# Decode attention with a Mish layer: w2 loaded into one buffer in eighteen loads, wo's last load moved ahead of the last values

## The chip, the cores and the metric

The kernel runs on one core of a Trainium2 chip. The metric is the device time of one execution in microseconds (us); lower is better. Three runs of the kernel before gave a median of 1326.32 us (1326.3 to 1327.66). The profile is of one more execution, of 1326.37 us, on the same core.

## The reference, cut to what matters

The input is one token for each of eight sequences (x is 8 x 512). It is normalised, and then goes through two branches whose results are added to it.

```python
xn = layernorm(x)                                    # 8 x 512
# A: attention over a cache, 32 query heads, 8 key/value heads, 8192 positions, head size 128
q = (xn @ wq).reshape(8, 32, 128)
p = softmax(q . k_cache / sqrt(128))                 # four query heads share one k/v head
a = (p . v_cache).reshape(8, 4096) @ wo              # wo: 4096 x 512
# B: a dense layer, Mish, a dense layer
h = xn @ w1 + b1                                     # 8 x 1792
b = (h * tanh(softplus(h))) @ w2                     # w2: 1792 x 512
out = x + a + b
```

All arrays are float32. The caches hold 2 x 268 MB, the four weight matrices 24 MB together. Each byte is read once.

## The kernel before, in words

**The stream of loads.** Nearly everything that the kernel reads goes through one pool `kv` of four buffers of 128 partitions x 32 KiB (4 MiB; `buffer()`, line 87). A list `items` (lines 605 to 622) holds, in order, pairs of a load and the work on what it loaded. The loop at line 625 issues the load of the item three places ahead (`AHEAD`), then emits the work of the present item. All these loads are issued by SyncE (SP in the profile), in that order. A load into a buffer waits until the work on the buffer's previous content is done.

The framework gives each load one of eight completion semaphores, called lanes, in turn. A load on a lane follows the load eight before it on the same lane.

**The order of items.** The attention goes in 16 packs of four batch elements for one k/v head. Pack p's keys are loaded in four items of 4 MiB (`load_k`), interleaved with the values of pack p - 1 (`load_v`, 4 MiB each). wq comes in four items of 2 MiB spread over the run, w1 in one of 3.5 MiB near the start. wo comes in four items of 2 MiB (`wo_work`): the item for heads n and n + 1 (n = 0, 2, 4, 6) stands right behind a values item. At the end stand: the last keys, the values of pack 15 in four items (b = 0 to 3), wo's last item (n = 6), and w2 in three items of 2, 1 and 0.5 MiB, each with a buffer of its own.

**The work of an item.** `scores` multiplies keys by expanded queries (line 316). `maximum`, `weights` and `sums` make the softmax of a pack. `values` (line 385) multiplies weights by one values item, in two halves of 16 matmuls (line 394) with a `yield` between them, and then VectorE adds four column groups of the result into `os` (lines 404 and 406). `merge` (line 417) sums `os` over partitions on TensorE (line 421); for the last b of a pack VectorE writes the pack's part of `oT` (line 425). `outputs` (line 431) multiplies two heads' groups of `oT` by wo: 32 matmuls, each two passes in the profile (line 446), into PSUM tile M, and VectorE adds M to the accumulator `acc` (line 456). `mish` makes the activations `aT` early in the run. `down` (line 508) multiplies `aT` by rows of w2, four matmuls for each of 14 row blocks j, accumulated in PSUM tile H (line 512; two passes each as well). At the end VectorE adds H and `acc` into `res` (line 634), and SP stores it (line 635).

**Work put off.** `after(k, f)` has f run after k more steps, and a step is taken at each `yield`. So `merge` comes two steps after the second half of its values, and `outputs` three steps after its item. VectorE and TensorE run their instructions in the order in which they are emitted (lines 638 to 650).

**What the change and the prediction touch:** `load_w2` (130), `outputs` (431), `down` (508), `wo_work` (591), `w2_work` (598), the list of items (605 to 622).

Of the kernel before, what the change touches and what calls it, by code (L numbers as in the profile page):

```python
# [13 lines left out]
P = 128  # L14
B = 8
D = 512
HKV = 8
REP = 4
# [9 lines left out]
BW = 1024  # L28
# [4 lines left out]
Q = P // G  # L33
# [5 lines left out]
PACKS = HKV * NP  # L39
# [18 lines left out]
W2R = G * FT // 2 * FP // P  # L58
# [6 lines left out]
def kernel(  # L65
# [12 lines left out]
    nc = tc.nc  # L78
# [8 lines left out]
    def buffer():  # L87
        return kv.tile([P, NB * BW], F32, name="kv")

    def load_blocks(src, lo, n):  # L90

        _, rows, width = src.shape
        t = buffer()[:rows, : n * width].rearrange("p (j f) -> p j f", j=n)
        nc.sync.dma_start(t, src[lo : lo + n].rearrange("j p f -> p j f"))
        return t

    def batch_blocks(src, p, b):
        n, hb = divmod(p, NP)
        lo = ((hb * PB + b) * HKV + n) * NB
        return src[lo : lo + NB]  # L100

    def load_k(p, b):
        src = batch_blocks(kT, p, b)
        t = buffer()
        if p > 0:
            nc.sync.dma_start(
                t, src.rearrange("j p f -> (j p f)").rearrange("(p f) -> p f", p=P)
            )
            return t
        t = t.rearrange("p (j f) -> p j f", j=NB // KA)  # L110
        nc.sync.dma_start(
            t,
            src.rearrange("(j a) p f -> j (a p f)", a=KA).rearrange("j (p f) -> p j f", p=P),
        )
        return t

    def load_v(p, b):

        t = buffer().rearrange("p (s f) -> p s f", s=NH)
        nc.sync.dma_start(  # L120
            t,
            batch_blocks(v, p, b)
            .rearrange("(s j) p f -> s (j p f)", s=NH)
            .rearrange("s (p f) -> p s f", p=P),
        )
        return t

    w2_rows = w2.rearrange("j p f -> (j p) f").rearrange("(q i) f -> q (i f)", i=W2R)

    def load_w2(lo, hi):  # L130

        t = buffer()[:, : (hi - lo) * BW]
        nc.sync.dma_start(t, w2_rows[:, lo * BW : hi * BW])
        return t

    x_sb = const.tile([B, D], F32, name="x_sb")
# [5 lines left out]
    items = []  # L142
# [4 lines left out]
    M = psum.tile([P, 512], F32, name="m")  # L147
    H = psum.tile([P, 512], F32, name="h")
# [21 lines left out]
    acc = const.tile([P, P], F32, name="acc")  # L170
# [214 lines left out]
    def values(p, b, vt):  # L385


        o = O[b % 2]
        for s in range(NH):
            u = s * PB + b  # L390
            for k in range(W // W4 // G):
                for c in range(G):
                    j = G * k + c
                    nc.tensor.matmul(  # L394
                        o[Q * c : Q * c + W4 * REP, :],
                        PT[p][:, W4 * R * j + u : W4 * R * (j + 1) : U],
                        vt[:, s, 512 * j : 512 * (j + 1)],
                        start=(s == 0 and k == 0),
                        stop=(s == NH - 1 and k == W // W4 // G - 1),
                    )  # L400
            if s == 0:
                yield
        os = OS[p, b] = work.tile([P, DH], F32, name="os", bufs=3)
        nc.vector.tensor_scalar(os, o[:, :DH], isel[:, 0:1], None, op0=ALU.mult)  # L404
        for i in range(1, W4):
            nc.vector.scalar_tensor_tensor(  # L406
                os,
                o[:, DH * i : DH * (i + 1)],
                isel[:, i : i + 1],
                os,  # L410
                op0=ALU.mult,
                op1=ALU.add,
            )
# [3 lines left out]
    def merge(p, b):  # L417

        n, hb = divmod(p, NP)
        at = 168 + b * REP  # L420
        nc.tensor.matmul(M[:, at : at + REP], OS.pop((p, b)), hsel, start=True, stop=True)  # L421
        if b == PB - 1:
            if hb == 0:
                oT[n] = work.tile([P, REP, B], F32, name="oT", bufs=4)
            nc.vector.tensor_mul(  # L425
                oT[n][:, :, hb * PB : (hb + 1) * PB],
                M[:, 168 : 168 + REP * PB].rearrange("p (b h) -> p h b", h=REP),
                RT.pop(p),
            )

    def outputs(n, w):

        if n == 0:

            for g in range(G):
                nc.tensor.matmul(
                    M[Q * g : Q * g + B, 256:384],
                    ident[:B, :B],
                    x_sb[:, g * P : (g + 1) * P],
                    start=True,  # L440
                    stop=False,
                )
        for h in range(2 * REP):
            for g in range(G):
                at = h % 2 * D + g * P
                nc.tensor.matmul(  # L446
                    M[Q * g : Q * g + B, 256:384],
                    oT[n + h // REP][:, h % REP, :],
                    w[:, h // 2, at : at + P],
                    start=(h == 0 and n > 0),  # L450
                    stop=(h == 2 * REP - 1),
                )
        if n == 0:
            nc.vector.tensor_copy(acc, M[:, 256:384])
        else:
            nc.vector.tensor_add(acc, M[:, 256:384], acc)

    def mish(w1_sb):

# [48 lines left out]
    def down(lo, hi, w):  # L508
        for j in range(2 * lo, 2 * hi):
            for g in range(G):  # L510
                at = (j - 2 * lo) * D + g * P
                nc.tensor.matmul(  # L512
                    H[Q * g : Q * g + B, :P],
                    aT[:, j, :B],
                    w[:, at : at + P],
                    start=(j == 0),
                    stop=(j == 2 * W2R - 1),
                )
# [4 lines left out]
    def after(k, f):  # L523
        late.append([k, f])
# [9 lines left out]
    def wq_item(i):  # L534
        def spread(n):
            return spread_q(n, KR, NB, qc[:, n % 4])

        def work_on(t):
            for n in (2 * i, 2 * i + 1):
                project(n, t)  # L540
            if i == 0:
                spread_q(0, KA, KA, qc0)()
                spread(0)()
                spread(1)()
            else:
                even = spread(2 * i)

                def then():
                    even()
                    after(1, spread(2 * i + 1))  # L550

                after(2, then)
            yield

        return lambda: load_blocks(wq, i * CC, CC), work_on
# [5 lines left out]
    def k_work(p, b):  # L561
        def work_on(t):
            if (p, b) == (0, 0):
                expand(0)
            yield from scores(p, b, t)
            if b == 0 and p + 1 < PACKS:
                expand(p + 1)
            if b == PB - 1:

                def largest():  # L570
                    maximum(p)
                    after(1, exponents)

                def exponents():
                    lsel = weights(p)
                    after(3 if p < PACKS - 1 else 2, lambda: sums(p, lsel))

                after(3 if 0 < p < PACKS - 1 else 2, largest)
            yield

        return work_on

    def v_work(p, b):
        def work_on(t):
            yield from values(p, b, t)
            after(2, lambda: merge(p, b))
            yield

        return work_on

    def wo_work(n):
        def work_on(t):
            after(3, lambda: outputs(n, t))
            yield

        return work_on

    def w2_work(lo, hi):
        def work_on(t):
            down(lo, hi, t)  # L600
            yield

        return work_on

    setup()
    items.append(wq_item(0))
    for i in range(PB * PACKS + PB):
        p, b = divmod(i, PB)
        if p < PACKS:

            if b == 2 and p % (2 * NP) == 2 and p < PACKS - NP:
                items.append(wq_item(p // (2 * NP) + 1))
            if i == 2:
                items.append((lambda: load_blocks(w1, 0, 2 * CC), w1_work))
            items.append((lambda p=p, b=b: load_k(p, b), k_work(p, b)))
        if p > 0:
            items.append((lambda p=p, b=b: load_v(p - 1, b), v_work(p - 1, b)))
            if i > PB and (i - PB + 1) % (2 * NP * PB) == 0:
                n = (p - 1) // NP - 1
                items.append((lambda n=n: load_blocks(wo, n * 2, 4), wo_work(n)))  # L620
    for lo, hi in ((0, 4), (4, 6), (6, 7)):
        items.append((lambda lo=lo, hi=hi: load_w2(lo, hi), w2_work(lo, hi)))

    tiles = {}
    for i in range(-AHEAD, len(items)):
# [12 lines left out]
    last = {}  # L638
# [50 lines left out]
```

## Time and profile before

| | |
|---|---|
| median of three runs | 1326.32 us |
| the profiled execution | 1326.37 us |
| its span, first to last instruction | 1324.6 us |
| TensorE clock granted, mean | 0.974 |
| read from memory | 561 MB, 424 GB/s over the span |
| TensorE busy | 1194.0 us, 90% |
| VectorE busy | 230.8 us, 17% |

In the profile PE is TensorE's matmuls, PEld its weight loads, DVE VectorE, ACT ScalarE, and SPq the issues of SP. A timeline row has its start in us from the span's start, the time from the first start to the last end, the engine, the line, the operation, what it writes and reads, and the count; in brackets stands how long the engine was idle before it, and what ended that. Rows of the chain of waits have a start, a length and what the time went to. A row of a window has its length, each engine's busy time with its count of instructions, TensorE's granted clock, DMA's busy share and GB/s. A row of a DMA queue has packets, MB and its share of the sixteen engines' time.

### The profile page before, as it was taken

Reading aid. Unit: us, or ns where it says so; the run is one execution under the profiler, and the core shown is the slowest. Engines: PE = TensorE matmul, PEld = TensorE weight load, DVE = VectorE, ACT = ScalarE, POOL = GpSimd, SP = SyncE. Lnnn points to the kernel's source line nnn. Section 1 sums busy time; section 2 is a strip of 40 time slices with the busy share of each in tenths; the row PEclk is TensorE's granted clock in tenths of the full one; section 3 lists DMA queues with packets and bytes.
Section 4 is the critical chain, followed back from the end, with each engine's and each line's share of the span. In section 5 each row is a group of like instructions: output and inputs, shape, how many; then the busy total and the mean of one; then the engine's idle time right before and its main releaser. Section 6 shows DMA issues by size and latency. Waiting matters only on the chain.

```text
span 1324.6 us, 11226 instructions
## 1 busy us (share of the span) xinstructions
PE 1194.0 (90%) x5096; PEld 498.4 (38%) x5096; DVE 230.8 (17%) x620; ACT 24.6 (2%) x39; POOL 8.7 (1%) x10
## 2 busy tenths in 40 slices
PE   4999989998979998999998999899898898999885
PEld 3233344433334434333333434443343343333322
DVE  4320211202021021110201111120110201202021
ACT  1000000000000000000000000000000000000000
POOL 2000000000000000000000000000000000000000
PEclk9999989999989998999998999899999899999988
DMA  9999999999999999999999999999999999999997
GB/s 383 425 434 424 431 429 427 431 427 428 430 426 428 433 426 433 427 426 430 431 427 429 427 427 428 429 430 432 427 428 425 425 430 431 427 433 426 428 428 295
DMA packets 34071, 561.80 MB, mean 424 GB/s; under 512 B 2268, under 2 KB 2400, under 8 KB 7656
## 3 DMA queue, kind: packets, MB, share of 16 engines
q1 hardware_dynamic: 34000, 561.06, 99.5%
q8 instruction: 40, 0.66, 0.2%
q14 instruction: 7, 0.06, 0.0%
q10 hardware_dynamic: 24, 0.02, 0.0%
HBM read 561.01 MB, written 0.07 MB: 424 GB/s over the span
## 4 chain that ended last, share of the span: by engine, by line
PE 52%; DMA 46%; DVE 1%; issue 0%; ACT 0%; ACTq 0%
DMA kv<-in_kT 44%; PE s L316 41%; PE o L394 6%; DMA kv<-in_w 2%; PE h L252 1%; PE s L304 1%; PE m L446 1%; PE h L512 0%; DVE e L188 0%; PE m L421 0%; PE h L229 0%; DVE qs L242 0%; PE m L359 0%; DVE pt L367 0%; DVE oT L425 0%
## 5 line engine op out<-in xcount | busy, mean ns | idle before, releaser
L316 PE MATMUL s<-kv,qT 128*128 128x512 f32 x1920 | 874.2, 609 | 81.3 <-DMA kv<-in_kT 81.3
L316 PEld LDWEIGHTS s<-kv,qT 128*128 128x128 f32 x1920 | 361.8, 194 | 532.8 <-issue 452.6
L394 PE MATMUL o<-kv,pt 128*16 128x512 f32 x2048 | 239.2, 606 | 14.5 <-DMA kv<-in_v 9.7
L404 DVE TENSOR_SCALAR os<-o,isel 128x128 f32<-128x128 f32 x64 | 22.4, 351 | 600.3 <-PE o L394 600.3
L394 PEld LDWEIGHTS o<-kv,pt 128*16 128x16 f32 x2048 | 59.2, 111 | 168.6 <-issue 151.6
L406 DVE SCALAR_TENSOR_TENSOR os<-o,isel,os 128x128 f32<-128x128 f32 x192 | 67.3, 350 | 6.8
L327 DVE TENSOR_REDUCE nm<-s 128x1 f32<-128x1024 f32 x16 | 19.6, 1225 | 208.9 <-PE s L316 206.2
L366 ACT ACTIVATE e<-s,nmx 128x1024 f32<-128x1024 f32 x16 | 17.8, 1114 | 1204.3 <-DVE nmx L361 1204.3
L421 PEld LDWEIGHTS m<-hsel,os 128*128 128x128 f32 x128 | 23.6, 192 | 39.3 <-issue 29.8
L367 DVE STREAM_TRANSPOSE pt<-e 128x1024 f32<-128x1024 f32 x16 | 32.2, 2010 | 21.2 <-ACT e L366 21.2
L304 PE MATMUL s<-kv,qT 128*64 128x512 f32 x128 | 30.7, 639 | 2.5 <-DMA kv<-in_kT 1.4
L277 DVE TENSOR_SCALAR qT<-qc,bsel 128x128 f32<-128x128 f32 x120 | 30.6, 339 | 0.0
L421 PE MATMUL m<-hsel,os 128*128 128x4 f32 x128 | 19.3, 221 | 6.5 <-DVE nr L338 4.8
L252 PE MATMUL h<-psel,qs 128*128 128x32 f32 x132 | 19.5, 307 | 3.6 <-DVE qs L242 3.6
L252 PEld LDWEIGHTS h<-psel,qs 128*128 128x128 f32 x132 | 19.6, 229 | 7.3 <-DVE qs L242 4.4
L304 PEld LDWEIGHTS s<-kv,qT 128*64 128x64 f32 x128 | 10.0, 147 | 22.3 <-issue 20.0
L381 DVE RECIPROCAL r<-m 128x16 f32<-128x16 f32 x16 | 4.1, 257 | 71.4 <-PE m L377 71.4
L259 DVE COPY qc<-h 128x256 f32<-128x256 f32 (+1 forms) x9 | 3.6, 402 | 55.5 <-PE h L252 55.5
L202 PE MATMUL m<-ident,e 8*128 8x8 f32 x4 | 0.6, 247 | 12.4 <-DVE e L200 12.4
L242 DVE TENSOR_SCALAR qs<-h 128x1024 f32<-128x1024 f32 (+1 forms) x9 | 10.2, 1130 | 3.4 <-PE h L229 3.4
L229 PE MATMUL h<-kv,xnT 128*8 128x128 f32 x256 | 9.4, 309 | 0.3 <-DVE xnT L205 0.3
L425 DVE TENSOR_TENSOR oT<-m,r 128x16 f32<-128x16 f32 x16 | 2.7, 171 | 38.1 <-PE m L421 38.1
(80 smaller groups left out, 119.5 us busy)
## 6 DMA issues: line engine op xcount, KB each, us to landing
kv<-in_kT SPq DMA_DIRECT2D x64, 4096.0 KB, 24.7
kv<-in_v SPq DMA_DIRECT2D x64, 4096.0 KB, 30.0
kv<-in_wq SPq DMA_DIRECT2D x4, 2048.0 KB, 19.5
kv<-in_wo SPq DMA_DIRECT2D x4, 2048.0 KB, 20.1
kv<-in_w SPq DMA_DIRECT2D x1, 3584.0 KB, 36.6
kv<-in_w SPq DMA_DIRECT2D x1, 2048.0 KB, 24.9
kv<-in_w SPq DMA_DIRECT2D x1, 1024.0 KB, 16.8
kv<-in_w SPq DMA_DIRECT2D x1, 512.0 KB, 8.0
```

The costliest lines, as they stand in the source:

```text
L252: nc.tensor.matmul(H[:, r * R : (r + 1) * R], qs[:, r].rearrange("p g i -> p (g i)"), psel.rearrange("p h b -> p (h b)"), start=True, stop ...
L277: nc.vector.tensor_scalar(t[:, :, :, lo : lo + R - U + 1 : U], q, bsel[:, j : j + 1], None, op0=ALU.mult)
L304: nc.tensor.matmul(sp[WK * z : WK * (z + 1), cols], t[:, w : w + WK], k[:, NH * s + z, at : at + 512], start=(b == 0 and s == 0 and i == 0 ...
L316: nc.tensor.matmul(sp[:, cols], t[:, w : w + P], k[:, at : at + 512], start=(b == 0 and r == 0), stop=(b == PB - 1 and r == KR - 1),)
L327: nc.vector.tensor_reduce(NM[p], sp, axis=AX.X, op=ALU.max, negate=True)
L366: nc.scalar.activation(e, S[p % 2], AF.Exp, bias=nmx, accum_out=l)
L367: nc.vector.transpose(pt.rearrange("p (m t r) -> p t m r", m=m, t=TG), e.rearrange("p (t q m) -> p t m q", t=TG, m=m),)
L394: nc.tensor.matmul(o[Q * c : Q * c + W4 * REP, :], PT[p][:, W4 * R * j + u : W4 * R * (j + 1) : U], vt[:, s, 512 * j : 512 * (j + 1)], sta ...
L404: nc.vector.tensor_scalar(os, o[:, :DH], isel[:, 0:1], None, op0=ALU.mult)
L406: nc.vector.scalar_tensor_tensor(os, o[:, DH * i : DH * (i + 1)], isel[:, i : i + 1], os, op0=ALU.mult, op1=ALU.add,)
L421: nc.tensor.matmul(M[:, at : at + REP], OS.pop((p, b)), hsel, start=True, stop=True)
L446: nc.tensor.matmul(M[Q * g : Q * g + B, 256:384], oT[n + h // REP][:, h % REP, :], w[:, h // 2, at : at + P], start=(h == 0 and n > 0), st ...
```

## The change

Four things change, all at the end of the list of items.

- w2 is one item with one buffer. It is loaded by eighteen loads: the first 3/7 of each partition's row (1.5 MiB in all) in sixteen loads of eight partitions each, the next 3/7 in one load of 128 partitions, the last 1/7 in another.
- Where wo's last item stood behind the last values item, it stands ahead of it.
- wo's last products are not put off by three steps. They are emitted between w2's first and second part.
- They are accumulated in H, with w2's products, and not in M; the addition of M to `acc` for them goes.

```diff
-    def load_w2(lo, hi):
-
-        t = buffer()[:, : (hi - lo) * BW]
-        nc.sync.dma_start(t, w2_rows[:, lo * BW : hi * BW])
+    W2_PARTS = ((0, 3), (3, 6), (6, 7))
+
+    def load_w2():
+
+        t = buffer()[:, : W2R * BW]
+        for lo, hi in W2_PARTS:
+            cols = slice(lo * BW, hi * BW)
+
+            step = 8 if lo == 0 else P
+            for q in range(0, P, step):
+                nc.sync.dma_start(t[q : q + step, cols], w2_rows[q : q + step, cols])
         return t
...
     def outputs(n, w):
 
+        last = n == HKV - 2
+        to = H[:, :P] if last else M[:, 256:384]
...
                 nc.tensor.matmul(
-                    M[Q * g : Q * g + B, 256:384],
+                    to[Q * g : Q * g + B, :],
                     oT[n + h // REP][:, h % REP, :],
                     w[:, h // 2, at : at + P],
-                    start=(h == 0 and n > 0),
-                    stop=(h == 2 * REP - 1),
+                    start=(h == 0 and 0 < n and not last),
+                    stop=(h == 2 * REP - 1 and not last),
                 )
...
-        else:
-            nc.vector.tensor_add(acc, M[:, 256:384], acc)
+        elif not last:
+            nc.vector.tensor_add(acc, to, acc)
...
+    wo_last = []
+
     def wo_work(n):
         def work_on(t):
-            after(3, lambda: outputs(n, t))
+            if n == HKV - 2:
+                wo_last.append(t)
+            else:
+                after(3, lambda: outputs(n, t))
             yield
...
-    def w2_work(lo, hi):
-        def work_on(t):
+    def w2_work(t):
+        for lo, hi in W2_PARTS:
             down(lo, hi, t)
             yield
+            if lo == 0:
+
+                outputs(HKV - 2, wo_last[0])
...
-            items.append((lambda p=p, b=b: load_v(p - 1, b), v_work(p - 1, b)))
             if i > PB and (i - PB + 1) % (2 * NP * PB) == 0:
                 n = (p - 1) // NP - 1
-                items.append((lambda n=n: load_blocks(wo, n * 2, 4), wo_work(n)))
-    for lo, hi in ((0, 4), (4, 6), (6, 7)):
-        items.append((lambda lo=lo, hi=hi: load_w2(lo, hi), w2_work(lo, hi)))
+                wo_item = (lambda n=n: load_blocks(wo, n * 2, 4), wo_work(n))
+                v_item = (lambda p=p, b=b: load_v(p - 1, b), v_work(p - 1, b))
+                items += [wo_item, v_item] if p == PACKS else [v_item, wo_item]
+            else:
+                items.append((lambda p=p, b=b: load_v(p - 1, b), v_work(p - 1, b)))
+    items.append((load_w2, w2_work))
```

In `down` the column of a block j of w2 is counted from the start of the whole row, not of a part. The emitted order of TensorE at the end is then: the third values item of pack 15 and its merge, the last values item, w2's first part (24 matmuls), the last merge, wo's last products (32), w2's second part (24) and its third (8).

More of the change, by code (lines that the diff above doesn't have):

```diff
@@ L446, in outputs @@
                 nc.tensor.matmul(
-                    M[Q * g : Q * g + B, 256:384],
+                    to[Q * g : Q * g + B, :],
                     oT[n + h // REP][:, h % REP, :],
                     w[:, h // 2, at : at + P],
-                    start=(h == 0 and n > 0),
-                    stop=(h == 2 * REP - 1),
+                    start=(h == 0 and 0 < n and not last),
+                    stop=(h == 2 * REP - 1 and not last),
                 )
         if n == 0:
-            nc.vector.tensor_copy(acc, M[:, 256:384])
-        else:
-            nc.vector.tensor_add(acc, M[:, 256:384], acc)
+            nc.vector.tensor_copy(acc, to)
+        elif not last:
+            nc.vector.tensor_add(acc, to, acc)
     def mish(w1_sb):
@@ L510, in down @@
             for g in range(G):
-                at = (j - 2 * lo) * D + g * P
+                at = j * D + g * P
                 nc.tensor.matmul(
@@ L589, in v_work @@
         return work_on
+    wo_last = []
     def wo_work(n):
         def work_on(t):
-            after(3, lambda: outputs(n, t))
+            if n == HKV - 2:
+                wo_last.append(t)
+            else:
+                after(3, lambda: outputs(n, t))
             yield
         return work_on
-    def w2_work(lo, hi):
-        def work_on(t):
+    def w2_work(t):
+        for lo, hi in W2_PARTS:
             down(lo, hi, t)
             yield
-        return work_on
+            if lo == 0:
+                outputs(HKV - 2, wo_last[0])
     setup()
```

## The prediction

> **What bounds the kernel now.** I read the page's sections 1 to 4 first, then the chain of waits over the last 40 us, then the order in time of TensorE and of SP's issues there.
>
> ```profile
> span 1324.6 us, 11226 instructions
> PE 1194.0 (90%) x5096; PEld 498.4 (38%) x5096; DVE 230.8 (17%) x620; ACT 24.6 (2%) x39; POOL 8.7 (1%) x10
> ...
> DMA  9999999999999999999999999999999999999997
> ...
> q1 hardware_dynamic: 34000, 561.06, 99.5%
> q8 instruction: 40, 0.66, 0.2%
> q14 instruction: 7, 0.06, 0.0%
> q10 hardware_dynamic: 24, 0.02, 0.0%
> HBM read 561.01 MB, written 0.07 MB: 424 GB/s over the span
> ```
>
> The sixteen DMA engines are busy in every slice but the last, and SP's queue q1 takes 99.5% of their time: one stream of 561 MB at 424 GB/s. TensorE is 90% busy but waits for data whenever it has caught up. The change touches neither the bytes nor anything ahead of the last dozen loads, so it can win or lose only at the end of the stream.
>
> ```profile
> 1290.20 24.92 DMA kv<-in_w
> 1315.12 0.04 issue
> 1315.16 4.41 PE h L512 x96
> 1319.57 1.75 PE m L446 x64
> 1321.32 0.49 PE h L512 x16
> 1321.81 0.02 issue
> 1321.83 0.29 DVE res L634
> ```
>
> The chain ends on w2's first load (issued at 1290.20, landed at 1315.12). Behind it stand 6.65 us of TensorE work, then the result's addition and store. What can be gained is a part of these 6.65 us.
>
> ```profile
> 1295.38 3.20 PE L394 MATMUL o<-kv,pt 128*16 128x512 f32 x16 [5.24 <-DMA kv<-in_v]
> ...
> 1305.19 3.41 PE L394 MATMUL o<-kv,pt 128*16 128x512 f32 x16 [4.44 <-DMA kv<-in_v]
> 1308.53 0.39 PE L421 MATMUL m<-hsel,os 128*128 128x4 f32 x2
> 1308.85 1.93 PE L394 MATMUL o<-kv,pt 128*16 128x512 f32 x16
> 1312.40 0.39 PE L421 MATMUL m<-hsel,os 128*128 128x4 f32 x2 [1.63 <-DVE os L406]
> ```
>
> The last two values loads release TensorE at 1295.38 and 1305.19. The last one's products end at 1310.78. From the last values to w2's first part, 1305.19 to 1315.16, the stream moves wo's 2 MiB and 2 MiB of w2: 4.98 us for each 2 MiB.
>
> **The change, part by part.**
>
> *wo ahead of the last values.* wo takes the place of the last values in the queue and the other way round; both have their buffers in time, as SP's issues show (the pair ends at 1274.80, the next goes at 1285.86; by then the second last values and wo are still ahead, some 14 us of transfer).
>
> ```profile
> 1270.49 4.31 SPq L120 DMA_DIRECT2D kv<-in_v  x2
> ...
> 1285.86 0.37 SPq L94 DMA_DIRECT2D kv<-in_wo  x1
> 1290.20 20.96 SPq L133 DMA_DIRECT2D kv<-in_w  x3
> ```
>
> So the last values land one wo later: 1305.19 + 4.98 = **1310.17**. Their products take 3.41 + 1.93 = 5.34 us; the merge that stood between the halves moves forward into the wait for the values and costs nothing there (TensorE is idle from 1302 on). They end at 1315.5, 4.7 us later than now. This is the price of the move. What it buys: wo's products (1.75 us) no longer need anything late, and w2's products no longer start on a TensorE that has idled: now 96 take 4.41 us, 46 ns each, while the 64 behind them take 1.75, 27.3 ns each.
>
> *One buffer and sixteen pieces.* All 18 loads of w2 share one buffer, free at 1290.20. By the three rows above they could queue at once, 15 us before they are needed. But the compiled order of the changed kernel shows a wait on the DMA lanes (there are eight, taken in turn, and a load waits for the one eight before it on its lane):
>
> ```
> 135 L94 DMACopy kv<-in_wo 128x4x1024 [waits DMAHW5_49,PE_49]
> 136 L120 DMACopy kv<-in_v 128x2x4096 [waits DMAHW6_49,PE_49]
> 137 L140 DMACopy kv<-in_w 8x3072 [waits DMAHW7_49,PE_49]
> 138 L140 DMACopy kv<-in_w 8x3072 x4
> 139 L140 DMACopy kv<-in_w 8x3072 [waits DMAHW0_49]
> 140 L140 DMACopy kv<-in_w 8x3072 [waits DMAHW1_49]
> 141 L140 DMACopy kv<-in_w 8x3072 [waits DMAHW2_49]
> ```
>
> Counting pieces 0 to 15, piece 5 waits for the second last values, piece 6 for wo, and **piece 7 for the last values**. SP issues in order, so pieces 7 to 15 and w2's other two loads, 11 issues, all stand behind 1310.17. On SP nothing but the store is queued behind them; who waits is TensorE. That the stream is then empty for about a microsecond is new.
>
> The price of an issue: the nearest rows are SP's three w2 loads now and ACT's two small loads of eight and four partitions.
>
> ```profile
> L133 SPq DMA_DIRECT2D kv<-in_w x3: 328/341/341, 1290.2 to 1310.8; - x3
> ...
> 0.74 0.43 SPq L94 DMA_DIRECT2D kv<-in_wq  x1
> 1.23 1.04 SPq L111 DMA_DIRECT2D kv<-in_kT  x2
> ...
> 0.73 0.60 ACTq L137 DMA_DIRECT2D x_sb<-in_x  x1
> 1.37 0.26 ACTq L139 DMA_DIRECT2D b_sb<-in_b  x1
> ```
>
> With the 0.06 us gap between SP's first two issues, the ends are 0.26 + 0.06 = 0.32 and 0.60 + 0.06 = 0.66 us a piece. I take 0.40, from SP's own 0.34.
>
> The price of a piece's transfer: q10 carried just those two small loads, and its 24 packets are 8 + 4 rows and 8 + 4 completions. So a load of eight partitions runs on eight engines: 12 KiB each, at 424 / 16 = 26.5 GB/s 0.46 us. The store of the result gives the fixed part:
>
> ```profile
> out<-res SPq DMA_DIRECT2D x1, 64.0 KB, 1.6
> ```
>
> 64 KB on sixteen engines landed 1.6 us after the issue, so a lone piece (0.3 us more data per engine) lands after 1.9. Piece 7 goes out at 1310.2 and lands at 1312.1; eight more at 0.46 (more than the 0.40 of an issue) land by **1315.8**. With 0.66 us an issue it is 1310.2 + 8 x 0.66 + 1.9 = 1317.4.
>
> *The tail, summed.* The values' products end at 1315.5, the pieces are there at 1315.8, eight lanes are waited for at one instruction (0.2 us allowed): w2's first 48 products start at 1316.0 and end 48 x 27.3 ns later, 1317.3. The last merge is ready 1.62 us after the values' products (now 1310.78 to 1312.40), at 1317.1, hidden by them; 0.39 us, to 1317.7. wo's 64 products, 1.75 us, to 1319.45; the first half doesn't need the merge, which hides the 0.17 us multiplication behind it. w2's second load is issued at 1310.2 + 9 x 0.40 = 1313.8; on the engines that carry pieces it follows them: 1315.8 + 1.57 MB / 424 GB/s (3.7) = 1319.5. One more thing falls here: instruction fetches.
>
> ```profile
> q8 instruction: 1, 0.02, 2.7%
> ```
>
> This is the row of fetches among the DMA's of 1316 to 1318.5 now: one fetch, when TensorE has entered w2's products, on an engine with little left to do. TensorE reaches the same instructions at 1316 in the changed kernel, when every engine is in w2's second load. A fetch holds its engine for 0.2% x 16 x 1324.6 / 40 = 1.06 us; a load lands with its slowest engine. On an engine without pieces: 1313.8 + 1.6 + 3.5 (3.7 less what the 1.6 holds) + 1.06 = **1320.0**. So the second 48 products run 1320.0 to 1321.3, w2's third load (0.52 MB, 1.24 us) lands at 1321.25, the last 16 products (0.49) end at 1321.8. Now they end at 1321.81. **The sum is a change of 0.0 us**, with 0.1 for rounding up waits: the profiled execution's 1326.37 us (span 1324.6 and 1.8 around it; the three timed runs' median is 1326.32) becomes **1326.5 us**. The addition of wo's products to the accumulator, which goes, was hidden beside w2's last 16 products and gives nothing.
>
> **A rule against it.** The Trainium skill, "DMA: Bandwidth & Descriptors", section "Rules for kernel authors", asks for an outer dimension that is a multiple of 16, since one of fewer than 16 confines a load to that many engines. The section "Why a DMA increments its semaphore by 16 and not by 1" adds that SP's loads take the lowest-numbered ones. The packets of q10 agree with the first; which engines they are, no row shows. Spread over all sixteen by that rule, a piece would take 0.23 us, all would land by 1315.2, and the products, which wait for the values until 1315.5, would start 0.3 us sooner (an estimate). It is the third rival below.
>
> **The rivals.** About 0.2% (2.65 us) is what a measurement of this kernel can tell from no change; the bounds of the chances are 1323.7 and 1329.0.
>
> 1. *The lane waits and the fetch are hidden, and TensorE's own order is the bound.* From 1315.5: 1.31, the merge to 1317.5, 1.75, 1.31, 0.49: 1321.1, so -0.7 us, **1325.6**. For it: pieces and products meet within 0.3 us. Against: w2's second load is then needed at 1319.3, and by its rate alone comes at 1319.5. If the pieces were all queued early (the lane waits not being what I read), it is the same time, for the values land no sooner. Chance 0.28.
> 2. *SP's issues become the bound (the slower side).* At 0.66 us an issue w2's second load goes out at 1316.1 and lands at 1322.3 with the fetch, the third at 1323.6: end 1324.1, **1328.7**. Over 0.70 us an issue it is slower by over 0.2%; at 0.85 it is 1330.4. For it: ACT's 0.60 for eight partitions. Against: that was ACT's first, and four partitions took 0.26. Chance 0.15, half of it beyond 1329.
> 3. *The pieces fall on the late engines.* Engines finish apart: in 1310 to 1312 only 65% are busy, at 256 GB/s, while w2's first part is not yet down.
>
> ```profile
> 1308.00:1310.00 2.00, 2.00 (x18) 0.72 (x18) 0.00 (x0) 0.00 (x0) 0.00 (x0) 0.93 0.99 412
> 1310.00:1312.00 2.00, 0.77 (x8) 0.00 (x0) 1.05 (x3) 0.00 (x0) 0.00 (x0) 1.00 0.65 256
> ```
>
> If the eight engines with pieces are those that bring the last values last, pieces 0 to 6 (7 x 0.46 = 3.2 us) still stand there at 1310.2: all land by 1317.6 + 0.4, w2's others at 1321.7 and 1322.95, or 1.06 later with a fetch: **1328.1 to 1329.2**. Chance 0.10.
> 4. *The last values come earlier than by a whole wo*, since the late engines are what sets their landing and something relieves them: 3 us of that would make **1323.5**. No row shows what would. Chance 0.05.
>
> **How the numbers follow.** Forecast 0.42, rivals 0.28, 0.15, 0.10, 0.05. The likeliest is 1326.5; its own spread, 1325.9 to 1327.4. The range for 8 in 10 takes in rival 1 and most of 2 and 3: **1325.2 to 1329.3**. Faster by over 0.2%: rival 4 and little else, 0.05. Slower: half of rival 2, a third of 3, and 0.06 for prices that I have too low: 0.17. Within 0.2%: 0.78.
>
> **What would show it.** In the changed profile: TensorE waits for the last values until about 1310.2 instead of 1305.2; SP's small loads stand in two groups, the later one starting when the last values land, about 0.4 us apart; DMA's share drops around 1311; w2's products run at about 27 ns each; the last wait before the end is on w2's second load. Wrong would be: all sixteen pieces issued near 1290; issues over 0.7 us apart; last values before 1309; any difference ahead of 1290, where the two kernels issue the same loads.

## The result and the profile after

Four runs of the changed kernel have a median of **1337.72 us** (1336.93 to 1339.03), four runs of the kernel before on the same chip 1326.31 us (1326.24 to 1327.66): a ratio of 1.0084, 95% interval 1.0072 to 1.0097. The forecast was 1326.5 us, with no change as the likeliest case; the measured time is 8 us above its range. The profiled execution took 1338.47 us, so its terms stand 0.75 us above the median.

The head and the end of section 3 of the page after:

```profile
span 1336.7 us, 11241 instructions
...
HBM read 561.01 MB, written 0.07 MB: 420 GB/s over the span
```

The same bytes in a span that is 12.1 us longer (1336.7 less 1324.6). Up to 1290 the windows of the two kernels agree (DMA's GB/s to within 1). All of the loss lies in the last 45 us, which the chain of waits shows (start, length, what):

```profile
1285.13 27.01 DMA kv<-in_v
1312.14 0.02 issue
1312.15 3.89 DMA kv<-in_w
1316.05 0.02 issue
1316.06 10.12 DMA kv<-in_w
1326.18 0.20 issue
1326.38 2.75 PE h L521 x48
1329.12 0.52 PE m L428 x2
1329.64 2.42 PE h L455 x64
1332.07 1.80 PE h L521 x64
```

The last values land at 1312.14 (forecast 1310.17). Then comes piece 7, which waited for them (issued at 1312.15, landed at 1316.05), then piece 15, which waited for piece 7's lane (issued at 1316.06, landed at 1326.18, forecast 1315.8). w2's first products start at 1326.38 (forecast 1316.0), and TensorE ends at 1333.87 (forecast 1321.8): 10.4 us too late at the pieces, another 1.7 in the products behind them.

SP's waits from 1300 on (total, times, longest) stand on the instructions that the prediction named:

```profile
SPq L140 <- DMA kv<-in_v: 11.4, 1, 11.4
SPq L140 <- DMA kv<-in_wo: 4.8, 1, 4.8
SPq L140 <- DMA kv<-in_w: 2.7, 4, 0.8
```

One piece waits for wo, one for the last values, and all behind it with them. The last row is new: pieces 14 and 15 and w2's other two loads also waited for pieces 6 to 9, which should have been down long before, and so the last issues stand 0.8 to 1.1 us apart.

The windows show why. The columns are those of the prediction's rows; the last two are DMA's busy share and GB/s.

```profile
1303.00:1306.00 3.00, 0.39 (x2) 0.30 (x2) 0.21 (x1) 0.00 (x0) 0.00 (x0) 1.00 0.92 225
1306.00:1309.00 3.00, 0.00 (x0) 0.00 (x0) 0.00 (x0) 0.00 (x0) 0.00 (x0) 0.65 0.66 232
...
1312.00:1316.00 4.00, 3.82 (x20) 0.84 (x24) 0.00 (x0) 0.00 (x0) 0.00 (x0) 0.50 0.49 104
1316.00:1318.00 2.00, 2.00 (x16) 0.29 (x8) 0.00 (x0) 0.00 (x0) 0.00 (x0) 0.72 0.40 74
...
1320.00:1326.00 6.00, 0.00 (x0) 0.00 (x0) 0.00 (x0) 0.00 (x0) 0.00 (x0) 0.54 0.95 158
```

The first of these windows in the kernel before:

```profile
1303.00:1306.00 3.00, 0.81 (x4) 0.16 (x8) 0.00 (x0) 0.00 (x0) 0.00 (x0) 0.81 1.00 416
```

Read the last two columns together. From 1303 to 1306 the engines are 92% busy and move 225 GB/s, where the kernel before moved 416 at 100%. A busy engine that moves half as much isn't short of work: each of its packets takes longer. The trace's packet records show it: the values' packets of 16 KiB take 0.61 us in the kernel before, and in the changed kernel 0.90 us at the median of those that start from 1302 to 1304 and 1.17 from 1304 to 1306. From 1312 to 1318 only pieces are in flight, and six to eight engines (0.40 to 0.49 of sixteen) move 104 and 74 GB/s, not the eight times 26.5 = 212 GB/s of the prediction. The question for the experiments was what stretches the packets.

### The profile page after: what moved, and what is told of

The parts are those of the page before. It is cut to its first block, busy times and chain, and to the rows that moved or that the text cites. A ratio compares the mean times of both kernels' runs of the same rounds, so it can differ in the third digit from the quotient of the medians.

```text
span 1336.7 us, 11241 instructions
## 1 busy us (share of the span) xinstructions
PE 1188.6 (89%) x5096; PEld 495.9 (37%) x5096; DVE 230.5 (17%) x619; ACT 24.6 (2%) x39; POOL 8.7 (1%) x10
## 4 chain that ended last, share of the span: by engine, by line
PE 50%; DMA 47%; DVE 1%; issue 0%; ACT 0%; ACTq 0%
DMA kv<-in_kT 44%; PE s L323 40%; PE o L401 6%; DMA kv<-in_v 2%; PE h L259 1%; PE s L311 1%; DMA kv<-in_w 1%; PE m L455 0%; DVE e L195 0%; PE m L428 0%; PE h L521 0%; PE h L236 0%; DVE qs L249 0%; PE h L455 0%; PE m L366 0%
## 5 line engine op out<-in xcount | busy, mean ns | idle before, releaser
L521 PE MATMUL h<-kv,aT 128*8 128x128 f32 x112 | 4.7, 335 | 8.1 <-DMA kv<-in_w 8.1
```

## The experiments

Three theories of the stretched packets: each **small load** costs about a microsecond, or eight engines do worse than sixteen, whatever is loaded; the **rows read** lie too near each other in memory; the **partitions written** decide, by the ports of the SBUF (the on-chip memory of 128 partitions) that they reach. Beside them stood the question of what the other parts of the change cost alone. Unless another base is named, each edit replaces the line of `load_w2` that issues the pieces, of which this is the core:

```diff
-            for q in range(0, P, step):
-                nc.sync.dma_start(t[q : q + step, cols], w2_rows[q : q + step, cols])
```

### Without pieces: three loads of 128 partitions

```diff
+            nc.sync.dma_start(t[:, cols], w2_rows[:, cols])
```

> The changed kernel without the pieces: w2's first part in one load of 128 partitions, so w2 is three loads into one buffer and no lane is waited for. It tells what the rest of the change (one buffer, wo ahead of the last values, its products between w2's) is worth. All theories: the last values land at 1310.2, w2's parts by 1314 to 1319, and TensorE's own order is the bound: 1325.6 us, between 1325.2 and 1326.6. If the move of wo itself costs what the changed kernel lost, over 1329.

Measured: 1326.22 us, ratio 0.9998 (0.9988 to 1.0008). Its timeline of TensorE:

```profile
1310.06 5.32 PE L399 MATMUL o<-kv,pt 128*16 128x512 f32 x32 [6.58 <-DMA kv<-in_v]
1315.21 1.48 PE L519 MATMUL h<-kv,aT 128*8 128x128 f32 x48
...
1317.34 1.93 PE L453 MATMUL h<-kv,oT 128*8 128x128 f32 x64
1319.09 1.93 PE L519 MATMUL h<-kv,aT 128*8 128x128 f32 x64
```

These are the prediction's numbers nearly to a tenth: values at 1310.0, their products 5.3 us, w2's first 48 products behind them without a wait, the end at 1321.0 where the first rival had 1321.1. (The profiled execution, 1325.62 us, is the fastest of the ten; the median is 0.6 us above it.) One buffer, wo's move and the order of the products together cost and gain nothing that these runs can tell. The whole loss belongs to the sixteen pieces.

### Both sides spread: every sixteenth partition and its row

```diff
+                for q in range(16):
+                    nc.sync.dma_start(t[q:P:16, cols], w2_rows[q:P:16, cols])
```

> The changed kernel, with each small load taking every sixteenth partition (and the rows that belong there) instead of eight neighbours; everything else as in the changed kernel, the result too. Theory P (a load into eight neighbouring partitions is slow on the SBUF side, for they share a write port or two): a piece takes about 0.5 us, the last values land at 1310.2, the pieces by 1315.8, and the time is 1326 to 1327 us. Theory H (eight neighbouring rows of w2 are slow to read from memory): the same, 1326 to 1327. Theory K (a load on eight engines costs over 1 us wherever it goes, one after another): as the changed kernel, 1337 to 1339.

Measured: 1338.68 us, 1.0091 (1.0076 to 1.0106). It is no better than the changed kernel. The values landed at 1313.76, later still, and SP took 0.56 us for each issue instead of 0.30. Of the three theories only the first expected this; spreading as such is no cure.

### One side at a time: sixteenths

```diff
+                    nc.sync.dma_start(t[8 * q : 8 * q + 8, cols], w2_rows[q:P:16, cols])
```

> Small loads into eight neighbouring partitions, as in the changed kernel, but from every sixteenth row of w2: the rows stand in the wrong partitions, so w2's first part is permuted; the work is the same. P: as slow as the changed kernel, 1337 to 1339 us, pieces 1.0 to 1.5 us apart. H: 1326 to 1327, pieces 0.4 to 0.5 us apart. K: 1337 to 1339.

```diff
+                    nc.sync.dma_start(t[q:P:16, cols], w2_rows[8 * q : 8 * q + 8, cols])
```

> The reverse: small loads from eight neighbouring rows of w2 into every sixteenth partition (w2's first part permuted, the work the same). P: 1326 to 1327 us, pieces 0.4 to 0.5 us apart. H: 1337 to 1339, pieces 1.0 to 1.5 us apart. K: 1337 to 1339.

Measured: 1336.24 us, 1.0074 (1.0054 to 1.0094), for neighbouring partitions with spread rows, and 1338.83 us, 1.0094 (1.0073 to 1.0114), for spread partitions with neighbouring rows. The intervals overlap, all three kernels are as slow as the changed one, and nothing is told apart. What remained possible was that sixteenths are a poor spread on one of the two sides.

### Both sides by fours

The port map of the Trainium skill ("SBUF — State Buffer", section "Door 1: The DMA port swizzle") says that four neighbouring partitions share a port, partitions 32 apart share it too, and partitions 64 apart do not. By this map eight neighbours reach two ports of sixteen, every sixteenth partition four, and every fourth within 32 eight, as many as a load of eight partitions can. So the next step was four.

```diff
+                for q in range(16):
+                    at = 32 * (q // 4) + q % 4
+                    four = slice(at, at + 29, 4)
+                    nc.sync.dma_start(t[four, cols], w2_rows[four, cols])
```

> The small loads take every fourth partition of a group of 32, with the rows that belong there; the result is unchanged. After the first four kernels K has fallen in its simple form, since single pieces passed in 0.46 us where few engines had any, and H and P stand amended. P2 (the eight engines of a piece write into too few write ports: neighbours reach two, every sixteenth partition four, every fourth one eight): a piece's packets take 0.46 us, the last values land at 1310 to 1311, the pieces about 0.6 us apart by 1317, time 1326.5 to 1328.5. H2 (eight rows read at once from one small part of w2, or at a bad distance): no better than every sixteenth row, 1336 to 1339. K2 (eight engines of one half, whatever they touch, pass about 100 GB/s together): 1336 to 1339, packets of 0.75 to 1.1 us.

Measured: 1331.59 us, 1.0037 (1.0023 to 1.0052): six microseconds of the loss are gone, and five remain: the port theory's 1326.5 to 1328.5 us was too low. Its timeline of TensorE and SP:

```profile
1310.10 5.18 PE L406 MATMUL o<-kv,pt 128*16 128x512 f32 x32 [6.70 <-DMA kv<-in_v]
1316.08 0.91 SPq L145 DMA_DIRECT2D kv<-in_w  x2
1320.30 2.75 PE L526 MATMUL h<-kv,aT 128*8 128x128 f32 x48 [5.02 <-DMA kv<-in_w]
```

The values land on time again (1310.05), although pieces 0 to 6 still stand among them. The packets of the early pieces take 0.46 us, just as the prediction had it. With this the theory that small loads or eight engines are slow in themselves falls as the cause of these six microseconds: these are loads of the same number and size.

### One side at a time: fours

Here `near` stands for the eight neighbours, `slice(8 * q, 8 * q + 8)`.

```diff
+                    nc.sync.dma_start(t[four, cols], w2_rows[near, cols])
```

> Every fourth partition, from eight neighbouring rows (w2's first part permuted, the work the same). P2: packets of 0.46 us, 1326.5 to 1328.5. H2: 1336 to 1339. K2: 1336 to 1339.

```diff
+                    nc.sync.dma_start(t[near, cols], w2_rows[four, cols])
```

> Eight neighbouring partitions, from every fourth row (w2's first part permuted, the work the same). P2: 1335 to 1339, packets of 0.7 to 1.1 us. H2: 1326 to 1328. K2: 1336 to 1339.

Measured: with partitions by fours and neighbouring rows 1332.33 us, 1.0043 (1.0028 to 1.0059); with neighbouring partitions and rows by fours 1338.37 us, 1.0090 (1.0069 to 1.0110). The values' products in the first:

```profile
1309.99 5.44 PE L406 MATMUL o<-kv,pt 128*16 128x512 f32 x32 [6.43 <-DMA kv<-in_v]
```

and in the second:

```profile
1312.58 6.41 PE L406 MATMUL o<-kv,pt 128*16 128x512 f32 x32 [8.45 <-DMA kv<-in_v]
```

Only the partitions matter for the landing of the values. Wherever the rows come from, partitions by fours leave the values at 1310.0, and neighbours make them 2.6 us late. The time of the first is again above the 1326.5 to 1328.5 us expected. The theory of the rows falls.

### Fewer pieces, none behind the last values

```diff
+            cuts = (0, 8, 16, 24, 32, P) if lo == 0 else (0, P)
+            for q, r in zip(cuts, cuts[1:]):
+                nc.sync.dma_start(t[q:r, cols], w2_rows[q:r, cols])
```

> Only the first 32 partitions of w2's first part come in small loads, four of eight neighbours; the other 96 in one. So no load of w2 waits for the last values: they are queued by 1300.5. It parts the lane waits from the slow transfers. If the slow transfers alone delay the last values: they land 0.5 to 1.5 us after 1310.0, the end is that much later than with three loads, 1326.5 to 1328. If the lane waits make the loss and early pieces are harmless: 1325.6 to 1326.6, as with three loads. If slow pieces cost as much when they are queued early: over 1330.

```diff
+                for q in range(4):
+                    nc.sync.dma_start(t[q:32:4, cols], w2_rows[q:32:4, cols])
+                nc.sync.dma_start(t[32:, cols], w2_rows[32:, cols])
```

> Beside the kernel with four early pieces of neighbours: the same four pieces and the same load of the other 96 partitions, but each piece takes every fourth of the first 32 partitions, so that it reaches eight ports; the result is unchanged. P2 with the four pieces as the culprits: the last values land at 1310.0 to 1310.5, 1325.7 to 1327.5 us. If the load of 96 partitions is itself slow: over 1330, but with the last values earlier than 1316.1, since the pieces no longer slow them.

With five loads ahead, no load of w2 waits for the last values: all are issued by 1300.3. Measured all the same: 1336.19 us, 1.0073 (1.0058 to 1.0088), with four pieces of neighbours, and 1333.82 us, 1.0056 (1.0042 to 1.0070), with four by fours. A window of the first, in the middle of the transfer:

```profile
1306.00:1309.00 3.00, 0.00 (x0) 0.00 (x0) 0.00 (x0) 0.00 (x0) 0.00 (x0) 0.50 0.96 206
```

All sixteen engines are busy and move half of what they can, with the last values among it (they land at 1316.08, and at 1314.86 in the second). So the lane waits are not needed for the loss. Four good pieces help by 2.4 us at most: that is the difference of the medians, and the two intervals overlap. Both results are over 1330 with the values earlier in the second, which was the expectation for the case that the load of 96 partitions is itself slow, although it reaches every port.

### Whole width, narrow columns: the lane waits alone

```diff
+            step = 192 if lo == 0 else (hi - lo) * BW
+            for at in range(lo * BW, hi * BW, step):
+                nc.sync.dma_start(t[:, at : at + step], w2_rows[:, at : at + step])
```

> The lane waits alone. w2's first part again in sixteen loads, but each of all 128 partitions and 192 columns; the result is unchanged. So loads 7 to 15 and the two behind them again wait for the last values, but each reaches every write port. Theory P2 (write ports make the loss): the last values land at 1310.0, the sixteen parts by 1315 to 1316, and the time is that of the prediction's sum, 1325.8 to 1327.5 us. If the lane waits have a price of their own beyond that sum: over 1328.5.

Measured: 1329.38 us, 1.0021 (1.0010 to 1.0031). There are still eighteen loads, with the same waits for lanes, but each goes to all 128 partitions. TensorE and the row of instruction fetches among the DMA's of 1312 to 1325:

```profile
1315.20 1.48 PE L521 MATMUL h<-kv,aT 128*8 128x128 f32 x48
...
1322.53 2.38 PE L521 MATMUL h<-kv,aT 128*8 128x128 f32 x64 [3.26 <-DMA kv<-in_w]
```

```profile
q8 instruction: 2, 0.03, 0.9%
```

The first part of w2 is in time. What is late is its second load: fourteen engines had it down by 1320.16, one at 1321.36, one at 1322.49. The prediction had 1319.5 without a fetch and 1320.0 with one. Two fetches fall into this window, but by the packet records the second starts at 1324.08, after the landing; only the first, 0.93 us from 1318.80, is ahead of it. So one fetch, as in the prediction, and it can have held one of the two late engines. The records don't name the engine of a packet, and what held the other stays open. The loads here also have packets of 768 bytes, so 3.0 us is an upper price for the lane waits.

### wo's place, and a version without it

Three loads again, and wo back behind the last values:

```diff
-                items += [wo_item, v_item] if p == PACKS else [v_item, wo_item]
+                items += [v_item, wo_item]
```

> The changed kernel without pieces (w2 in three loads into one buffer) and without the move of wo: wo's load again behind the last values, its products still between w2's parts. By the prediction's sum the last values land at 1305.2, w2's parts at 1313.7, 1317.4 and 1318.6, and TensorE starts w2's products cold at 1313.7: end 1319.8 to 1320.5 against 1321.8, so 1324.3 to 1325.1 us. If only the order on TensorE counts and not what lands last: 1326.3.

The kernel before with w2 in one buffer and three loads (3/7, 3/7, 1/7), and wo's last products put off by one step instead of three:

```diff
-            after(3, lambda: outputs(n, t))
+            after(1 if n == HKV - 2 else 3, lambda: outputs(n, t))
```

> The kernel before with two things changed: w2 in three loads of 3/7, 3/7 and 1/7 into one buffer, and wo's products right behind the last merge, ahead of all of w2's. TensorE does wo's products while w2's first part lands (1312.8 to 1315.2, cold), then w2's as they come, the last at 1318.6: end 1319.2 to 1319.6, so 1323.6 to 1324.2 us. If the last load lands later than that, the end is 0.7 us behind its landing.

Measured: 1325.13 us, 0.9987 (0.9979 to 0.9996), and 1324.51 us, 0.9988 (0.9979 to 0.9996). Both intervals end below 1, and both gains are under the 0.2% that the prediction set as its bound. The two aren't told apart. In the second, TensorE goes from wo's products to all of w2's without a wait:

```profile
1314.14 3.58 PE L449 MATMUL m<-kv,oT 128*8 128x128 f32 x64 [0.27 <-DVE oT L428]
1317.48 3.32 PE L515 MATMUL h<-kv,aT 128*8 128x128 f32 x112
```

It has the lowest median of the versions measured here. By the medians wo's move ahead of the values is worth a loss of about 1 us (1326.22 against 1325.13, each beside its own 1326.4), though the intervals overlap: what it makes the values late by, 5.0 us, is not quite regained.

### Each pattern of partitions by itself

What stayed open was why the load of 96 partitions was slow, and whether the number of ports is all that counts: an engine may also have to write to the port which it serves in a load of 128 partitions. Loads added behind the output's store of the kernel before, each group between loads of 128 partitions that wait for it:

```diff
+    for q in range(0, 64, 8):
+        nc.sync.dma_start(probe[q : q + 8, :], rows[q : q + 8, :])
...
+    for q in range(8):
+        at = 32 * (q // 4) + q % 4
+        nc.sync.dma_start(probe[at : at + 29 : 4, :], rows[at : at + 29 : 4, :])
```

> The kernel before, with loads added after the store of the output: 2 MiB at a time (64 partitions by 32 KiB) in eight loads of eight partitions, or four of sixteen, or one, each group between loads of all 128 partitions (4 MiB) that wait for everything ahead of them. Only the added loads are read, each by the time from its first issue to its last landing; the total is the kernel before plus all of them and is not compared. If only the number of ports of the SBUF that a load reaches counts (a load of 64 partitions in one half reaches eight, eight neighbours two, every sixteenth four, every fourth eight), then every fourth partition takes about 10 us per 2 MiB in the lower half, in the upper half and shifted by four alike (eight engines at the 26.5 GB/s of the loads of values), the one load of 64 partitions as little, eight neighbours at a time and every sixteenth 15 to 40. If what counts is that an engine writes to the port which it also serves in a load of 128 partitions, then only every fourth of the lower half takes 10; the upper half and the shifted ones take 12 to 20, and the one load of 64 or 96 partitions is slow too. If the destination does not count when nothing else is in flight, all groups take about 10, and the loss in the changed kernel is one of transfers that stand in the way of each other.

SP's issues in the timeline. The lines are, in order: eight neighbours (L642), every fourth in the lower half (L646), in the upper half (L650), shifted by four (L654), every sixteenth (L657), sixteen neighbours (L660), one load of 64 (L662), one of 96 (L664); the odd rows between are the loads of 128.

```profile
1332.12 2.87 SPq L642 DMA_DIRECT2D kv<-in_kT  x8
1368.05 0.36 SPq L643 DMA_DIRECT2D kv<-in_kT  x1
1380.27 5.43 SPq L646 DMA_DIRECT2D kv<-in_kT  x8
1393.10 0.36 SPq L647 DMA_DIRECT2D kv<-in_kT  x1
1405.30 5.32 SPq L650 DMA_DIRECT2D kv<-in_kT  x8
1418.15 0.33 SPq L651 DMA_DIRECT2D kv<-in_kT  x1
1430.39 9.33 SPq L654 DMA_DIRECT2D kv<-in_kT  x8
1443.75 0.33 SPq L655 DMA_DIRECT2D kv<-in_kT  x1
1455.91 5.24 SPq L657 DMA_DIRECT2D kv<-in_kT  x8
1478.54 0.34 SPq L658 DMA_DIRECT2D kv<-in_kT  x1
1490.69 1.72 SPq L660 DMA_DIRECT2D kv<-in_kT  x4
1511.05 0.35 SPq L661 DMA_DIRECT2D kv<-in_kT  x1
1523.39 0.52 SPq L662 DMA_DIRECT2D kv<-in_kT  x1
1536.11 0.35 SPq L663 DMA_DIRECT2D kv<-in_kT  x1
```

Each group's time, in this one execution, is the next row's start less its own. The engines are counted from the completions of a load, and the last column is the median time of a packet of 32 KiB, both from the trace's packet records. For 2 MiB:

| partitions of a load | ports by the map | engines | us | packet, us |
|---|---|---|---|---|
| eight neighbours | 2 | 8 | 35.9 | 4.14 |
| every sixteenth | 4 | 8 | 22.6 | 2.51 |
| sixteen neighbours | 4 | 16 | 20.4 | 4.54 |
| every fourth: lower half, upper half, shifted by four | 8 | 8 | 12.8, 12.9, 13.4 | 1.21 in each |
| one load of 64 | 8 | 16 | 12.7 | 2.56 |
| one load of 128, for 4 MiB | 16 | 16 | 12.2 | 1.21 |

(Of the shifted loads the last four overlap the first four in four partitions and waited for them, so their 13.4 is not the rate alone.)

Windows inside the groups of eight neighbours, every fourth (lower half), every sixteenth, sixteen neighbours, and a load of 128:

```profile
1337.00:1366.00 29.00, 0.00 (x0) 0.00 (x0) 0.00 (x0) 0.00 (x0) 0.00 (x0) 0.50 0.47 59
1384.00:1392.00 8.00, 0.00 (x0) 0.00 (x0) 0.00 (x0) 0.00 (x0) 0.00 (x0) 0.50 0.49 201
...
1462.00:1477.00 15.00, 0.00 (x0) 0.00 (x0) 0.00 (x0) 0.00 (x0) 0.00 (x0) 0.50 0.48 101
1495.00:1510.00 15.00, 0.00 (x0) 0.00 (x0) 0.00 (x0) 0.00 (x0) 0.00 (x0) 0.50 0.88 101
...
1371.00:1379.00 8.00, 0.00 (x0) 0.00 (x0) 0.00 (x0) 0.00 (x0) 0.00 (x0) 0.50 1.03 446
```

Three rows have the same share, 0.47 to 0.49, half the engines, and move 59, 201 and 101 GB/s. The fourth has twice the engines busy and moves the same 101 as the third: it reaches as many ports. So neither the size of a load nor its number of engines sets the rate, but the number of ports: 59 / 2, 101 / 4, 201 / 8 and 446 / 16 are 30, 25, 25 and 28 GB/s a port. The figure of the Trainium skill, in the section cited above, is about 27 GB/s a port, and these rows agree with it. The packets say the same: with one engine to a port they take 1.21 us, with two about 2.5, with four 4.1 to 4.5. The theory that an engine must write to a port of its own falls for loads by themselves: the upper half and the shifted groups take as long as the lower half.

The load of 96 partitions was issued at 1548.36, and SP's last wait for it was 16.4 us: 16.8 us for 3 MiB. It reaches all sixteen ports, though eight of them get two thirds of its bytes: 2.1 MB at 8 x 25 to 28 GB/s are 9 to 11 us. The loads of 64 and of 128 took 1.3 and 2.8 us more than their bytes at the rate of their windows (184 and 446 GB/s), so 11 to 13 us would be the estimate, and 4 to 6 remain that the count doesn't explain. Its packets took 2.4 us at the median, twice those of the load of 128. That its engines meet at the same ports would fit, and wasn't tried.

## Why the prediction was wrong

**What was right.** Which load waits for which lane; that piece 7 and all behind it stand behind the last values; SP's issues of a piece (0.34 us apart, 0.40 taken); the merge moved into the wait (1303.27); that nothing ahead of 1290 changes. The run without pieces gave the rest of the sum within 0.2 us: values at 1310.0, their products 5.3, the end at 1321.0.

**The step that failed** is the price of a piece's transfer: "12 KiB each, at 424 / 16 = 26.5 GB/s 0.46 us". It took an engine's rate from loads of 128 partitions and asked only how many engines a piece has. A piece of eight neighbours writes through two ports; alone on the chip such loads moved 59 GB/s, so 98.3 KB take 1.67 us, and nine of them 15.0. Measured in the changed kernel, from piece 7's issue to the last landing: 1326.18 - 1312.15 = 14.0 us, against 5.6 forecast (1315.8 - 1310.2). That the two are so near is partly chance. Until 1318 the pieces overlap one another, their packets take about 1.05 us, and 104 and 74 GB/s are more than the 59 alone; from 1318 w2's second load goes beside them, and the packets of both take up to 1.5 us. With partitions by fours the step's own 0.46 us is what the early packets took.

**What came with it, and was not thought of:**

- The narrow loads also slow the wide ones beside them. Pieces 0 to 6 stand among the last values and wo, and the core moves 225 GB/s there; the values land 2.0 us late. In the prediction's sum these pieces cost the values nothing; only its third rival had early pieces stand in the way.
- TensorE idles until 1326.38, and its clock is granted at 0.50 from 1326 to 1330. w2's first 48 products take 2.75 us, 1.48 in the run without pieces; wo's 2.42 against 1.75. Against the forecast's terms the first 48 take 1.4 us more, the merge 0.1 and wo's products 0.7; less the 0.55 us of waiting for w2's second load that the forecast had there, this makes the 1.7 us behind the pieces. The prediction had seen such a cold start in the kernel before and counted it away, since it saw no wait ahead of w2's products.
- The lane waits cost up to 3.0 us by themselves (columns of 128 partitions), where the sum had them hidden: w2's second load is issued at 1314.09 (forecast 1313.8) and lands at 1322.49 instead of 1320.0, on two late engines, of which one fetch explains one at most.

**The parts of the 11.4 us**, each run beside its own runs of before: one buffer, move and order -0.2 (1326.22 less 1326.39, within the noise); the lane waits, with loads to all ports, up to +3.2 more (+3.0 in all); another 2.1 up to partitions by fours (+5.1), where SP's issues are longer and a load has eight engines and eight ports instead of sixteen, which no run parts; and 6.3 for the partitions' being neighbours. The last is shown by edits: with the rows left as they were, partitions by fours take away 5.6 of it (+5.8), although SP's issues become longer, 0.62 us against 0.30.

**The rules and rivals.** The rule that the prediction weighed, on the number of engines, was not the one that decided: twice the engines moved the same 101 GB/s. The rule that speaks against this change is the Trainium skill's port map, cited above, which the prediction did not weigh. By its figure of about 27 GB/s for each of two ports a piece takes 1.8 us, an estimate from that page of the Trainium skill, and nine pieces after the last values end at about 1328.5; the trace has 1326.18. The third rival (pieces on late engines) had the nearest mechanism, early pieces that stand in the way, but at the same 0.46 us a piece, and so a loss of 1.8 to 2.9 us. The second, SP's issues, was not the bound, for they are 0.34 us apart. In the run with fours on both sides they are 0.66 apart, and w2's second load goes out at 1316.08, as this rival had it; but that run took 1331.59 us, not 1328.7.

## What to carry to other kernels

In these runs a load's rate went by the ports that its destination reaches, with the load of 96 partitions as an exception on the slow side. So where a load has to be cut, cut it along the free dimension and keep all 128 partitions (here +3.0 us instead of +11.4); if it must be cut by partitions, take a step of four (+5.1), and reckon with SP's longer issue. A DMA share near 1 with half the usual GB/s was the sign of it, and the loads beside the narrow ones paid as well. And loads that are cut finer than the lanes allow wait for the loads ahead of them: eight more loads in the queue can undo an early issue.

## What the runs showed of the hardware

- SP's time for the issue of a load of eight partitions depends on their step: about 0.30 us for neighbours, 0.56 for every sixteenth, 0.62 for every fourth.
- A load of 96 partitions (3 MiB) took 16.8 us by itself, one of 128 (4 MiB) 12.2: the larger is the faster one, and the number of ports explains only part of it.
- By fours, the pieces issued behind the last values, nearly all in the upper half, had packets of 0.52 to 0.74 us at the median; those among the values, in the lower half, 0.46. Alone both halves took the same. The two groups differ in more than the half, and why the later ones are slower stays open.
- Packets of one size take longer the more engines share a port, by the map: 32 KiB in 1.21 us with one engine to a port, about 2.5 with two, 4.1 to 4.5 with four.
